# First two pairs of tiles from plain quadrants, keys and values as two offset streams, and weights split early: a gated mix of two linear attentions on one Trainium2 core

## The chip, the cores and the metric

The kernel runs on one core of one Trainium2 chip. The metric is the device time of one execution in microseconds. Engines are named as in the profile: PE (TensorE) multiplies, PEld loads its stationary operand, DVE (VectorE), ACT (ScalarE) and POOL (GpSimd) work on elements, and SP (SyncE) issues every transfer from one queue (SPq), in program order.

## The reference

A sequence of S = 2048 rows of D = 576 goes through two linear-attention blocks with 32 heads of 18, and a gate mixes the results. Block A maps queries and keys by elu + 1, block B by a learned projection and two softmaxes. Neither is causal, so each block needs one state over all rows (keys times values, and the sum of keys) before the first query can be answered.

```python
pq, pk = phi(q), phi(k)                  # A: phi(t) = (t > 0 ? t + 1 : exp(t)) + 1e-6
kv = einsum("bhsd,bhse->bhde", pk, v); z = einsum("bhsd->bhd", pk)
o = einsum("bhqd,bhde->bhqe", pq, kv) / (einsum("bhqd,bhd->bhq", pq, z)[..., None] + 1e-6)
a = o @ A_wo
pq, pk = q @ w_phi, k @ w_phi            # B: per head, then
phi_q = concat([softmax(pq), softmax(-pq)]); phi_k = concat([softmax(pk), softmax(-pk)])
...
g = sigmoid((x * gate_w).sum(-1, keepdims=True))
return g * a + (1 - g) * b
```

## The kernel before

The rows are cut into 16 tiles of 128, taken as 8 pairs. Matmuls run on fp32r operands; to keep fp32 precision each operand is split into a high part (an ACT copy) and a low part (a subtraction of that copy on DVE or POOL), and a product is made of high times high, high times low and low times high.

The work has three phases. Phase A projects keys and values of block A for pair 0 to 7 and adds each pair to the state in PSUM (`kv_a`, matmuls in L217). Phase B does the same for block B (`kv_b`). The query phase projects queries for both blocks, normalizes, transposes and makes the output (L156 projections, L652 numerators, L682 output).

Keys or values of a pair are made by a Winograd form of Strassen's scheme (`wino`, matmuls in L359): x and the weight are cut into 2 x 2 quadrants of 288, and seven products replace eight. A product is 7 matmuls of 128x288, so keys or values of one pair take 49. The price is in sums: `x_ops` makes four sums of quadrants per pair on DVE (L257 to L268) and splits seven operands (`x_op`: copy on ACT L237, subtractions on POOL L238 and L239); `w_ops` does the like for a weight (sums L313 to L322; `w_op`: L293 on ACT, L294 and L295 on DVE); and results are added back on DVE (L369).

W is a tile of 18 blocks of 1440 columns: seven blocks for keys, seven for values, and what is not yet used holds other things; the seven operands of pair 1 lie there at first. The operands of x (tiles xo, ten buffers of 640 columns) are written to DRAM when made (L274, `xd`) and read back in phase B (`x_back`, L286) by 56 loads of 320 KB.

The first pairs: x tiles and the four quadrants of the keys' weight are loaded in turn, `x_ops(0)`, `w_ops` and `x_ops(1)` are woven, then keys of pairs 0 and 1, then the values' weight, then values of both. From pair 2 on keys and values of a pair are woven product by product. In phase B the last two pairs do keys together, then `load_w` loads and splits the query weight of A (WAq, L121 to L124), then both pairs' values.

Then comes the change of phase: masked states `kta` (L504), the output weight of B loaded and split (L121 to L124), and `ma_units`, which multiplies A's state with A's output weight into MA (matmuls L540 and L543, high part on ACT L544, low part on DVE L546 and L548); these are woven with the query units of the first tile. Block B's state becomes `ktb`, z_b and kb (L702 to L725). In the query phase each tile adds 1 to its two gate columns on DVE (L558).

The framework's scheduler reorders instructions of each engine; `tc.high_priority(offset=AHEAD)` pulls the Winograd copies and adds ahead. The order on each engine is fixed when the kernel is built.

## Time and profile before

| | |
|---|---|
| median of 3 runs | 626.22 us (626.06 to 630.88) |
| the profiled execution | 630.87 us |
| its span in the trace | 629.2 us |
| mean granted clock of PE | 0.986 of full |
| busy: PE, DVE, ACT, POOL | 589.0, 490.5, 256.0, 244.4 us |

The profile shows one execution. The stretches of its trace are given from the start of the span; "granted clock" is the share of full speed (2.4 GHz) that the chip allowed PE in a stretch. A matmul's busy time holds its waiting in PE's pipeline, so full pace is read from how many matmuls a stretch holds, not from the mean of one.

### The profile page before, as it was taken

The page shows a single profiled execution, that of the slowest core. Times are in us where ns is not written, and L with a number is a line of the kernel's source. Part 1 is how long each engine was busy: PE and PEld are TensorE (multiplying, and loading weights), DVE is VectorE, ACT ScalarE, POOL GpSimd, SP SyncE. Part 2 cuts the span into 40 slices and gives each one's busy share as a digit, 9 for nine tenths or more (in the row PEclk, how much of TensorE's full clock was granted, in tenths as well). Part 3 has the DMA queues.
Part 4 walks back from the last instruction along what each step waited for, and adds up shares of the span by engine and source line. Part 5 has one row for each costly group of instructions (what it writes and reads, how often), then busy time and mean ns, then how long its engine had stood idle before and what let it go on. Part 6 is the DMA issues. An engine that isn't in the chain of part 4 may idle for free.

```text
span 629.2 us, 12059 instructions
## 1 busy us (share of the span) xinstructions
PE 589.0 (94%) x4786; PEld 570.5 (91%) x4786; DVE 490.5 (78%) x817; ACT 256.0 (41%) x541; POOL 244.4 (39%) x226
## 2 busy tenths in 40 slices
PE   2788999999999899998998799999999999999997
PEld 2778999999999899997887599999999999999997
DVE  5999564959678558676979986999899898989920
ACT  5456456556333333453333334343332434332331
POOL 5958764840022203469526212333234442322300
PEclk9799999999999899999999989999999999999999
DMA  8855666666855454143102000111010110000001
GB/s 303 292 202 203 257 220 203 207 213 220 272 168 178 120 160 155 46 133 94 45 18 78 22 22 20 41 41 41 20 41 21 41 41 20 20 20 20 13 26 39
DMA packets 29292, 67.56 MB, mean 107 GB/s; under 512 B 3232, under 2 KB 4384, under 8 KB 29236
## 3 DMA queue, kind: packets, MB, share of 16 engines
q1 hardware_dynamic: 29236, 66.79, 32.0%
q8 instruction: 38, 0.62, 0.4%
q14 instruction: 18, 0.15, 0.1%
HBM read 43.70 MB, written 23.07 MB: 106 GB/s over the span
## 4 chain that ended last, share of the span: by engine, by line
PE 69%; DVE 16%; DMA 2%; ACT 2%; POOL 1%; issue 1%; SPq 0%; DVEq 0%; POOLq 0%; ACTq 0%
PE yz L359 25%; PE pq L156 16%; PE bk L682 15%; PE tr L652 4%; PE bk L217 3%; PE tr L627 2%; DVE dd L577 1%; PE yz L340 1%; DVE row L180 1%; DVE row L576 1%; DVE gg L558 1%; DVE W L616 1%; PE tr L620 1%; DVE uw L203 1%; DVE mm L185 1%
## 5 line engine op out<-in xcount | busy, mean ns | idle before, releaser
L359 PE MATMUL yz<-W,xo 128*128 128x288 f32 (+1 forms) x1386 | 202.6, 303 | 14.0 <-ACT W L293 6.4
L359 PEld LDWEIGHTS yz<-W,xo 128*128 128x128 f32 (+1 forms) x1386 | 192.2, 194 | 17.9 <-ACT W L293 6.6
L156 PE MATMUL pq<-W,xh 128*128 128x288 f32 (+1 forms) x576 | 128.8, 305 | 3.0 <-DVE uw L193 2.4
L156 PEld LDWEIGHTS pq<-W,xh 128*128 128x128 f32 x576 | 96.1, 191 | 5.3 <-DVE uw L193 1.8
L156 PE MATMUL pq<-W,xl 128*128 128x288 f32 (+1 forms) x320 | 94.1, 299 | 0.0
L203 POOL TENSOR_TENSOR uw<-uw,rs 128x1152 f32<-128x1152 f32 x16 | 34.2, 2154 | 97.5 <-DVE rs L198 85.0
L682 PE MATMUL bk<-W,ath 128*128 128x288 f32 x288 | 64.1, 302 | 1.8 <-DVE W L616 1.5
L156 PEld LDWEIGHTS pq<-W,xl 128*128 128x128 f32 x320 | 61.0, 191 | 0.5 <-issue 0.4
L682 PE MATMUL bk<-W,vo 126*128 126x288 f32 x384 | 59.5, 297 | 0.0
L364 ACT ACTIVATE sc<-yz 128x288 f32<-128x288 f32 x96 | 37.6, 406 | 47.4 <-PE yz L359 44.0
L194 ACT ACTIVATE uw<-uw 128x1152 f32<-128x1152 f32 x32 | 37.2, 1164 | 47.1 <-DVE uw L193 47.0
L103 POOL TENSOR_TENSOR xl<-xraw,xh 128x640 fp32r<-128x640 f32 x16 | 25.8, 1614 | 78.4 <-ACT xh L102 78.3
L682 PEld LDWEIGHTS bk<-W,vo 126*128 126x128 f32 x384 | 53.4, 188 | 0.0
L369 DVE TENSOR_TENSOR row<-yz,sc 128x288 f32<-128x288 f32 x48 | 21.5, 450 | 40.5 <-PE yz L359 22.7
L563 POOL TENSOR_TENSOR row<-row,z_a 128x576 f32<-128x576 f32 x16 | 30.1, 1882 | 58.4 <-DVE row L180 58.4
L196 DVE TENSOR_REDUCE ss<-uw 128x64 f32<-128x1152 f32 x32 | 42.8, 1344 | 10.0 <-ACT uw L194 9.9
L682 PEld LDWEIGHTS bk<-W,ath 128*128 128x128 f32 x288 | 47.4, 189 | 2.3 <-ACT W L615 1.7
L682 PE MATMUL bk<-W,atl 128*128 128x288 f32 x160 | 47.5, 298 | 0.0
L238 POOL TENSOR_TENSOR xo<-xs,xo 128x256 fp32r<-128x256 f32 x28 | 26.9, 961 | 30.0 <-ACT xo L237 27.0
L652 PE MATMUL tr<-W,kb_h 126*126 126x256 f32 (+1 forms) x160 | 33.0, 285 | 1.9 <-DVE W L616 0.9
L569 POOL TENSOR_TENSOR row<-row,den 128x576 f32<-128x576 f32 x16 | 19.1, 1191 | 37.2 <-issue 16.9
L293 ACT ACTIVATE W<-st 128x864 fp32r<-128x864 f32 x28 | 25.6, 924 | 18.1 <-DVE st L313 5.2
(170 smaller groups left out, 1140.9 us busy)
## 6 DMA issues: line engine op xcount, KB each, us to landing
xo<-xd SPq DMA_DIRECT2D x50, 320.0 KB
xd<-xo SPq DMA_DIRECT2D x49, 320.0 KB
xr<-xq SPq DMA_DIRECT2D x16, 384.0 KB
xraw<-xT SPq DMA_DIRECT2D x16, 320.0 KB
out<-row SPq DMA_DIRECT2D x16, 288.0 KB
xd<-W SPq DMA_DIRECT2D x7, 320.0 KB
st<-wAk SPq DMA_DIRECT2D x4, 432.0 KB
st<-wAv SPq DMA_DIRECT2D x4, 432.0 KB
```

The lines of the kernel that those rows point to most:

```text
L103: eng.tensor_tensor(xl, raw, r(xh), op=ALU.subtract)
L156: PE.matmul(dst, xx[:, j, :], W[:, w, c0:c0 + n], start=(i == 0), stop=(i == len(steps) - 1))
L194: A.activation(uw, uw, AF.Exp)
L196: V.tensor_reduce(ss, uw.rearrange("p s (h d) -> p (s h) d", d=DH), op=ALU.add, axis=AX.X)
L203: eng.tensor_tensor(u3, u3, rs[:, :, None].to_broadcast([P, 64, DH]), op=ALU.mult)
L238: G.tensor_tensor(dst[:, 3:5], raw[:, 0:2], r(dst[:, 0:2]), op=ALU.subtract)
L293: A.activation(T[:, 0:3], raw, AF.Copy)
L359: PE.matmul(dst, x[:n, i], w[:n, j], start=(first and m == 0), stop=(m == 6), skip_group_check=True)
L364: A.activation(s, y, AF.Copy)
L563: G.tensor_tensor(zw, f[:, :D], z_a, op=ALU.mult)
L652: PE.matmul(dst, kk[:n, i, :w], uu[:n, i, :256], start=(m == 0), stop=(m == 5))
L682: PE.matmul(po[:, :HB], l, w, start=(i == 0), stop=(i == len(steps) - 1))
```

## The change

1. Keys and values of pairs 0 and 1 come from plain quadrants (`plain`, 8 block products of 7 matmuls per pair, 224 in all, line 425 of the changed kernel). `x_op` now splits two halves with one instruction per engine; four weight blocks for keys and four for values are split, their 32-row tail on POOL. The Winograd sums of the weights (`t_ops`) come after. For phase B only the first operand tiles of these pairs are stored; `x_late` loads x again and makes the others at steps 8 and 25.
2. From pair 2 on keys and values are two streams that step by one product each, values four steps behind (`LAG`). Other work hangs on numbered steps (`task`). x operands are three tiles of 1280 columns and one of 640 per pair, from four and two buffers; they come back by 24 loads of 640 KB and 8 of 320 KB.
3. `pre_split` loads and splits WAq and woB in phase B and stores both parts in DRAM (18 stores); at the end they are loaded straight into W. `kta` is made in phase B, and the units of MA stand in the steps of the last four values products, their low part made by POOL (L508, L510) from a second ACT copy. The gate's +1 goes from DVE to ACT, one scale of the last pair from POOL to DVE.

```diff
     def x_op(dst, raw):
-        A.activation(dst[:, 0:3], raw, AF.Copy)
-        G.tensor_tensor(dst[:, 3:5], raw[:, 0:2], r(dst[:, 0:2]), op=ALU.subtract)
-        G.tensor_tensor(dst[64:96, 2], raw[64:96, 2], r(dst[64:96, 2]), op=ALU.subtract)
+        A.activation(dst[:, :, 0:3], raw, AF.Copy)
+        G.tensor_tensor(dst[:, :, 3:5], raw[:, :, 0:2], r(dst[:, :, 0:2]), op=ALU.subtract)
+        G.tensor_tensor(dst[64:96, :, 2], raw[64:96, :, 2], r(dst[64:96, :, 2]), op=ALU.subtract)
...
+        return p1.tile([P, 1280], F32R, name="xo", bufs=4)
...
+    def x_late(i):
+        tiles = [xo_tile(), xo_tile(), xs_tile()]
+        r0, r1 = x_load(2 * i), x_load(2 * i + 1)
+        for t, raw in zip(tiles, sums(r0, r1)):
+            x_op(as_op(t), raw)
+        x_keep(i, tiles)
...
+    def plain(ops, ks, c, then=None):
...
+        for h in range(2):
+            ys = {}
+            for a in range(2):
+                for i in range(2):
+                    for t in range(2):
+                        if a == 0:
+                            ys[i, t] = y_tile()[:, :HB]
+                        x, w = ops[i][2 * t + a], T[2 * a + h]
+                        for m, (p, q) in enumerate(((0, 0), (0, 3), (1, 1), (1, 4), (3, 0), (4, 1), (2, 2))):
+                            n = 96 if p == 2 else P
+                            PE.matmul(ys[i, t], x[:n, p], w[:n, q], start=(a == 0 and m == 0), stop=(m == 6),
+                                      skip_group_check=True)
...
+                A.activation(MA[:, j, c], pm[:, :HB], AF.Copy)
+                mr = row_tile()[:, :HB]
+                A.activation(mr, pm[:, :HB], AF.Copy)
+                if j < 4:
+                    G.tensor_tensor(MA[:, 5 + j, c], mr, r(MA[:, j, c]), op=ALU.subtract)
...
+    def pre_split(src, hi, lo):
+        raw = wraw_tile()[:src.shape[0], :src.shape[1]]
+        nc.sync.dma_start(raw, src)
+        t = pw.tile([P, 2, 578], F32R, name="ws")[:src.shape[0], :, :src.shape[1]]
+        A.activation(t[:, 0], raw, AF.Copy)
+        G.tensor_tensor(t[:, 1], raw, r(t[:, 0]), op=ALU.subtract)
+        for k, m in enumerate((hi, lo)):
+            if m is not None:
+                a = t.shape[0] - m.shape[0]
+                nc.sync.dma_start(m, r(t[a:, k]))
...
-    weave(x_ops(0, o0, x00 + x01), w_ops(wa, AKS), x_ops(1, o1, x1))
-    weave(keys(0, o0, AKS, phi_elu), keys(1, o1, AKS, phi_elu))
-    weave(w_ops(w_raw(wAv), AVS))
-    weave(values(0, o0, AVS), values(1, o1, AVS))
...
+    x_op(as_op(o0[0]), x0[0])
+    w_op(4, ak[0], G)
+    x_op(as_op(o0[1]), x0[1])
+    w_op(5, ak[2], G)
+    for t, raw in zip(o1, x1):
+        x_op(as_op(t), raw)
+    w_op(2, ak[1], G)
+    w_op(10, ak[3], G)
...
+    weave(plain(plains, [4, 2, 5, 10], lambda i, t, h: row_half(cs[i][t], h)))
...
+    for n in range(n_all + LAG):
...
+        if n < n_all:
+            next(K)
+        if n % 7 == 3 and n + 4 < n_all:
+            x_next(*pair_of(n + 4))
+        m = n - LAG
...
+        if m >= 0:
+            next(V2)
+        for fn in events.pop(n, []):
+            fn()
...
-        V.tensor_scalar(gg, gg, 1.0, None, op0=ALU.add)
+        A.activation(gg, gg, AF.Copy, bias=1.0)
```

The start on PE, before: yz is the PSUM tile of a product, xo the operands of pair 0, W alone stands for a weight block with an operand of pair 1.

```order
L359 MATMUL yz<-W,xo 128x288 x7
L359 MATMUL yz<-W 128x288 x4
L359 MATMUL yz<-W,xo 128x288 x7
L359 MATMUL yz<-W 128x288 x4
L359 MATMUL yz<-W,xo 128x288 x7
L359 MATMUL yz<-W 128x288 x7
```

Products of the two pairs alternate there. The same place in the changed kernel: both operands of every plain matmul lie in W; bk is the state in PSUM.

```order
L425 MATMUL yz<-W 128x288 x224
L217 MATMUL bk<-row,vo 57x54 x10
L217 MATMUL bk<-row,vo 38x36
L217 MATMUL bk<-row,vo 57x54 x10
L217 MATMUL bk<-row,vo 38x36
L367 MATMUL yz<-W,xo 128x288 x42
```

The products of both pairs, keys and values, now stand in one run ahead of the first state update, and Winograd products begin with pair 2.

Phase B on SP in the changed kernel: loads of pairs 6 and 7 (xd6, xd7), with WAd and WBd the split weights.

```order
L298 DMA xo_2920<-xd6_0_1286 128x1280
L298 DMA xo_2921<-xd6_1_1288 128x1280
L298 DMA xs1_2923<-xd6_3_1292 128x640
L298 DMA xo_2922<-xd6_2_1290 128x1280
L298 DMA xo_3107<-xd7_0_1502 128x1280
L298 DMA xo_3108<-xd7_1_1504 128x1280
L298 DMA xs1_3110<-xd7_3_1508 128x640
L696 DMA W_95<-WAd_507 128x578 x2
L298 DMA xo_3109<-xd7_2_1506 128x1280
```

Where seven loads of 640 columns stood for a pair, there are three of 1280 and one of 640, with the weights' own loads behind and between them. On PE, around the first use of xo_3107, which takes the buffer of xo_2728:

```order
L367 MATMUL yz_2946<-W_95,xo_2728 128x288 x7
L367 MATMUL yz_3134<-W_95,xo_2920 128x288 x7
L367 MATMUL yz_3045<-W_95,xo_2922 128x288 x2
L367 MATMUL yz_3056<-W_95,xs1_2729 128x288 x7
L367 MATMUL yz_3045<-W_95,xo_2922 128x288 x5
L367 MATMUL yz_3225<-W_95,xo_3107 128x288 x7
```

Between the last reading of the old tile and the first of the new stand 21 matmuls; the load can go only after the first of these places and must be there at the second.

MA's matmuls on PE before (L540), among query projections (L156) and behind the work on block B's state (L721):

```order
L721 MATMUL tr<-row,ath 72x8
L721 MATMUL tr<-row,atl 72x8
L540 MATMUL tr<-wraw,ath 128x288 x4
L156 MATMUL pq<-W,xh 128x288 x2
L156 MATMUL pq<-W,xl 128x288
```

They come in pieces of one to eight with projections between them. In the changed kernel they are L500 and L503 (wraw is A's output weight; xraw, xh and xl hold the masked states):

```order
L500 MATMUL yz<-wraw,xraw 128x288 x4
L367 MATMUL yz<-W,xo 128x288 x7
L500 MATMUL yz<-wraw,xraw 128x288
L500 MATMUL yz<-wraw,xh 128x288
L500 MATMUL yz<-wraw,xraw 128x288
L500 MATMUL yz<-wraw,xh 128x288 x5
L367 MATMUL yz<-W,xo 128x288 x7
L367 MATMUL yz<-W,xs_3110 128x288 x7
L500 MATMUL yz<-wraw,xh 128x288 x2
L500 MATMUL yz<-wraw,xl 128x288 x2
L503 MATMUL yz<-wraw,xl 64x288 x4
```

They moved from behind the work on block B's state to the last values products, ahead of the first query projection.

## Rows read from the trace of the kernel before

**Rows 1.** The page: busy time (share of the span) and instructions by engine.

```profile
PE 589.0 (94%) x4786; PEld 570.5 (91%) x4786; DVE 490.5 (78%) x817; ACT 256.0 (41%) x541; POOL 244.4 (39%) x226
```

**Rows 2.** Stretches: length, then PE, PEld, DVE, ACT, POOL, PEclk, DMA, GB/s.

```profile
0.00:60.00 60.00, 40.22 (x238) 36.50 (x239) 51.46 (x70) 32.45 (x62) 41.11 (x65) 0.94 0.71 251
60.00:210.00 150.00, 146.20 (x1398) 142.24 (x1397) 106.48 (x175) 74.76 (x156) 59.63 (x72) 1.00 0.64 214
...
280.00:288.00 8.00, 6.57 (x46) 5.86 (x44) 7.68 (x12) 5.40 (x11) 7.08 (x5) 1.00 0.64 186
288.00:360.00 72.00, 64.14 (x495) 57.12 (x495) 60.17 (x123) 24.06 (x56) 37.85 (x25) 0.98 0.15 44
...
400.00:580.00 180.00, 179.10 (x1383) 178.87 (x1381) 163.57 (x274) 62.76 (x145) 59.72 (x38) 1.00 0.09 30
```

**Rows 3.** Stretches of 10 us, the same columns.

```profile
20.00:30.00 10.00, 6.68 (x26) 5.57 (x26) 9.83 (x12) 5.45 (x11) 9.14 (x12) 0.74 0.94 310
...
220.00:230.00 10.00, 10.00 (x77) 10.00 (x76) 3.43 (x7) 2.48 (x6) 0.00 (x0) 1.00 0.50 143
...
340.00:350.00 10.00, 7.07 (x28) 4.70 (x26) 9.94 (x24) 3.76 (x11) 4.32 (x3) 0.83 0.21 63
```

**Rows 4.** A stretch, matmuls of L359 alone: PE, PEld, PEclk, DMA, GB/s.

```profile
0.00:55.20 55.20, 35.29 (x196) 31.94 (x197) 0.94 0.70 246
```

**Rows 5.** Timeline of the start: start, duration, engine, line, [idle before].

```profile
0.81 0.38 SPq L243 DMA_DIRECT2D xr<-xq  x1
...
3.75 0.94 ACT L237 ACTIVATE xo<-xr 128x384 fp32r<-128x384 f32 x2 [1.67 <-DMA xr<-xq]
...
4.35 0.72 POOL L238 TENSOR_TENSOR xo<-xr,xo 128x256 fp32r<-128x256 f32 x1 [0.58 <-ACT xo L237]
...
5.16 0.45 POOL L239 TENSOR_TENSOR xo<-xr,xo 32x128 fp32r<-32x128 f32 x1
...
14.05 1.33 PE L359 MATMUL yz<-W 128*128 128x288 f32 x4 [5.17 <-ACT W L237]
...
23.66 0.53 PE L359 MATMUL yz<-W 128*128 128x288 f32 x2 [2.42 <-POOL W L238]
```

**Rows 6.** Groups by shape on POOL: busy us, mean ns of one, idle before.

```profile
L238 POOL TENSOR_TENSOR xo<-xs,xo 128x256 fp32r<-128x256 f32 x28 | 26.9, 961 | 30.0 <-ACT xo L237 27.0 <-POOL xo L239 1.9
...
L239 POOL TENSOR_TENSOR xo<-xs,xo 32x128 fp32r<-32x128 f32 x28 | 17.8, 635 | 2.2
```

**Rows 7.** Groups by shape on DVE, the same columns.

```profile
L294 DVE TENSOR_TENSOR W<-st,W 128x576 fp32r<-128x576 f32 x28 | 24.1, 860 | 10.7 <-ACT W L293 10.5
...
L203 DVE TENSOR_TENSOR uw<-uw,rs 128x1152 f32<-128x1152 f32 x16 | 22.9, 1431 | 0.2
...
L369 DVE TENSOR_TENSOR row<-yz,sc 128x288 f32<-128x288 f32 x48 | 21.5, 450 | 40.5 <-PE yz L359 22.7 <-ACT sc L364 17.6
...
L558 DVE TENSOR_SCALAR gg<-gg 128x2 f32<-128x2 f32 x16 | 16.8, 1052 | 0.0
...
L295 DVE TENSOR_TENSOR W<-st,W 32x288 fp32r<-32x288 f32 x28 | 16.0, 571 | 0.6
...
L268 DVE TENSOR_TENSOR xs<-xr,xs 128x384 f32<-128x384 f32 x8 | 6.9, 868 | 0.9 <-POOL xo L239 0.8
...
L546 DVE TENSOR_TENSOR W<-tr,W 128x288 fp32r<-128x288 f32 x8 | 3.5, 442 | 0.0
...
L504 DVE TENSOR_TENSOR ath<-bk,row 57x54 f32<-57x54 f32 x8 | 1.7, 212 | 4.0 <-POOL ath L493 3.9
```

**Rows 8.** Chain of waits from 270 to 380: start us, length us, what.

```profile
280.49 3.74 DMA xraw<-xT
```

**Rows 9.** Groups by shape on PE: the matmuls that make MA.

```profile
L540 PE MATMUL tr<-wraw,ath 128*128 128x288 f32 x28 | 9.6, 462 | 2.2 <-DVE W L546 1.2 <-DVE kb_l L725 1.0
...
L543 PE MATMUL tr<-wraw,atl 128*64 128x288 f32 x16 | 2.4, 419 | 0.0
...
L540 PE MATMUL tr<-wraw,atl 128*128 128x288 f32 x4 | 1.9, 556 | 0.0
```

More of the change, by code (lines that the diff above doesn't have):

```diff
@@ new lines, in tile_gated_mix, with pair_of, x_next @@
+    t1 = st_tile()
+    weave(t_ops(*[ak[k] for k in range(4)], AKS, t1, t1, ak[1], ak[2]))
+    ts = [st_tile() for _ in range(4)]
+    weave(t_ops(*[av[k] for k in range(4)], AVS, *ts))
+    pair_kv(0, kv_a)
+    later = list(range(2, NP))
+    ops, made = {}, {}
+    n_a = 7 * len(later)
+    n_all = n_a + 7 * NP
+    def pair_of(n):
+        return ("a", 2 + n // 7) if n < n_a else ("b", (n - n_a) // 7)
+    def x_next(ph, i):
+        if ph == "a":
+            tiles = xo_tiles()
+            ops[ph, i] = seven(tiles)
+            weave(x_ops(i, tiles))
+        else:
+            ops[ph, i] = x_back(i)
@@ new lines, in open_b, with bk_half @@
+    def open_b():
+        nonlocal px, pw
+        pa.release()
+        px = ctx.enter_context(tc.tile_pool(name="px", bufs=2, side="right", reuse_waits="tile"))
+        pw = tc.alloc_tile_pool(name="pw", bufs=2, side="right", reuse_waits="tile")
+    def bk_half(n):
+        if n == 0:
+            t1 = st_tile()
+            b11, b12, b21, b22 = folded
+            w_op(BKS[0], b11)
+            w_op(BKS[1], b21)
+            made["bk"] = t_ops(b11, b12, b21, b22, BKS, t1, t1, b12, b21)
+            for _ in range(2):
+                next(made["bk"])
+        else:
+            weave(made["bk"])
+            w_op(BKS[6], folded[3])
@@ new lines, in bv_load, with bv_part @@
+    def bv_load():
+        made["bv"] = {k: w_raw(wBv, k) for k in (0, 2, 1, 3)}
+    def bv_part(n):
+        bv = made["bv"]
+        if n < 2:
+            w_op(BVS[n], bv[2 * n])
+        if n == 1:
+            t1 = st_tile()
+            made["bvt"] = t_ops(*[bv[k] for k in range(4)], BVS, t1, t1, bv[1], bv[2])
+            next(made["bvt"])
+        if n == 2:
+            weave(made["bvt"])
+            w_op(BVS[6], bv[3])
+    px = pw = None
+    for k, i in enumerate(later):
+        task(7 * k + LAG + 2, lambda i=i: pair_kv(i - 1, kv_a))
```

327 lines of the change are left out of this document (180 added, 147 removed).

## The prediction

> **What bounds the kernel now.** I read the busy line of the page first [rows 1]. The reader is to see that TensorE (PE) is busy 589.0 of 629.2 us, so only 40 us of the span have no matmul in them, and that VectorE (DVE) comes next with 490.5. Then the stretches [rows 2]: from 60 to 210 us PE has 146.20 of 150.00, from 400 to 580 it has 179.10 of 180.00. Nothing is to be had there except by taking matmuls away. The loss lies in two places. From 0 to 60 us PE has 40.22, and from 288 to 360 us, between the last values product and the first output product, it has 64.14 of 72.00 while DVE has 60.17.
>
> Busy time hides a second loss, since a matmul that goes slowly is busy too. At 220 to 230 us there are 77 matmuls in 10.00 us [rows 3], 130 ns from one to the next; that is my full pace. The products of the first two pairs are 196 matmuls (two pairs, keys and values, 49 each) and are done at 55.20 us [rows 4]. At 130 ns they would take 25.5. So the start costs 29.7 us beyond its own matmuls, and it is the largest single thing a change can attack.
>
> The timeline of the start says why [rows 5]. The first transfer is issued at 0.81, the first copy begins at 3.75. At 14.05 PE has waited 5.17 us for the second pair's first x operand, which ScalarE (ACT) copies late, behind sums and weight blocks of the Winograd form, and at 23.66 it has waited 2.42 us for the POOL subtraction in L238. From 20 to 30 us there are only 26 matmuls, and the granted clock is 0.74 [rows 3]: between the levels 2.4 and 1.2 GHz, PE having waited just before.
>
> **The change part by part.** All terms are against the profiled execution, 630.87 us, which is the slowest of the three runs shown and 4.65 over their median of 626.22; 1.67 us of it lie around the span.
>
> *Start: -10 us.* The plain quadrants need no sums, but 224 matmuls in place of 196: +28 × 130 ns = +3.6 us. By the order of the changed kernel the first four groups of seven need one x tile each, tile after tile; from the fourth tile on the 196 matmuls that follow are free of POOL. So the end is the time of the fourth tile on POOL plus 25.5. An x tile is now one copy and two POOL subtractions over both halves. POOL's durations for half a tile are 0.72 and 0.45 us when DVE is idle [rows 5] and 0.961 and 0.635 on the mean [rows 6]. For both halves: from below 1.98 (0.72 and 0.45 differ by 0.27 for 128 more elements, so 0.18 of it is fixed; 512 elements make 1.26 and 256 make 0.72), from above 2 × (0.961 + 0.635) = 3.19. I take 2.4, nearer to the rows with DVE idle, since DVE has little to do before 10 us. The first copy ends at 3.75 + 0.94 = 4.69. Four tiles are 9.6, and the tails of two weight blocks on POOL (0.45 us for 128 elements, so about 0.8 for 288) 1.6: 15.9 us, with the bounds 12.6 (no tail in front) and 19.4. Then 25.5, and for a spell at the lower clock 1.7: the 0.74 from 20 to 30 cost 2.6 [rows 3], and I expect one that is shorter. This gives 43.1 against 55.2, so -12. I give 2 back to DVE, which has to make eight sums of weight blocks and split them behind the plain products. It has 51.46 us of work in the first 60 [rows 2], and 14 of them go or move later: 12 Winograd adds × 0.450 = 5.4; eight sums of x at up to 0.868 = 6.9; six tails × 0.571 = 3.4, less what contention keeps [rows 7]. About 37 us of work from 6 us on ends at 43 or 44, beside the last plain product: hidden, with nothing to spare. Range -13 to -4.
>
> The Trainium skill, page "SBUF — State Buffer", section "Who interferes with whom", says that a DVE instruction with two SBUF inputs contends with a GpSimd instruction that reads SBUF, and that the loser waits out the whole instruction. The rows agree that there is contention (0.72 alone, 0.961 on the mean), though the difference is 0.24 and not a whole DVE subtraction. By that rule the eight POOL subtractions would each wait for one DVE split; this is the second rival.
>
> *The middle, 60 to 288 us: 0.* The sums of the first two pairs come here, made late, with four more loads of x: 8 × 0.868 = at most 6.9 us on DVE, which has 106.48 of 150 [rows 2], so they are covered. Splitting the query and output weights early is nine ACT copies, nine POOL subtractions and 18 stores in phase B, where ACT and POOL are under half busy. If a store that waits for POOL holds SP's queue, the loads behind it are late; this is counted below. Range -3 to +5: PE has 3.8 us of idle to win, and +5 if DVE's late sums delay the Winograd adds.
>
> *Loads of phase B: +5.* Before, ten tiles of 640 columns came back by loads of 320 KB, and the order leaves some 90 matmuls or more between a tile's last reading and the first reading of its successor. Now four tiles of 1280 come back by 640 KB each. In the order of the changed kernel the tightest of the 24 loads has 21 matmuls to land in (the fence shows it: after the last row with xo_2728 come 7, 2, 7 and 5 others, then xo_3107), 2.7 us; two have 29 (3.8), one has 35 (4.6), the other 20 have 40 or more (5.2 and up). Landing: the first transfer, 384 KB, took 3.75 - 0.81 = 2.94 us [rows 5]; one of 320 KB took 3.74 from issue to landing with others in flight [rows 8]. At the 310 GB/s of the start [rows 3] 384 KB are 1.24 us of bytes, so 1.7 are fixed; 640 KB alone are then 1.7 + 2.1 = 3.8. From above, twice the 3.74 is 7.5. I take 4.8, one more us for a neighbour in flight, nearer to the row with the first transfer. The stalls are 2.1 + 2 × 1.0 + 0.2 = 4.3, and 0.7 for SP's queue, in which each load stands behind a wait for PE and behind the weight stores. Range +1 (3.8) to +28 (7.5: 4.8 + 2 × 3.7 + 2.9, and 13 on the other 20).
>
> *Between values and output, 288 to 360 us: -7.* PE has 7.86 us without a matmul here. From 340 to 350 us DVE is busy 9.94 of 10 and PE 7.07, at 0.83 of full clock [rows 3]: DVE sets the pace. The change takes from DVE the lo parts of MA (8 × 0.442 and two of the smaller form, 4.4), the eight masks of kta and three smaller (11 × 0.212 = 2.3), and in this stretch three or so of the gate adds (3 × 1.052 = 3.2). It puts one scale of uw on DVE (1.431). Together 8.5 less [rows 7]. The matmuls for MA, 9.6 + 1.9 + 2.4 = 13.9 us [rows 9], are not removed but stand earlier, behind the last keys product, where they cover the softmax of the last pair. PE's work is the same, so the gain is at most its idle time, 7.9, plus the 1.7 that the 0.83 cost, plus 1.4 of idle from 280 to 288 [rows 2]. I take most of the idle time. Range -11 to -2; if that cover is not needed, because query projections covered it before, only a DVE chain made shorter by 2 remains.
>
> *Gate adds in the query phase: -0.5.* The other 13 × 1.052 us leave DVE, but PE is busy 179.10 of 180.00 there [rows 2]; ACT, under half busy, takes them. Range 0 to -2.
>
> Sum: -10 + 0 + 5 - 7 - 0.5 = -12.5, so 618.4 us for an execution like the profiled one, and 613.7, say 614, for the median.
>
> **The rivals.**
> 1. *The loads starve PE (slower).* If a 640 KB load takes 7.5 us, twice the 3.74, the term for phase B is +28 and not +5: 614 + 23 = 637. For it: the 3.74 was measured where 186 GB/s were moved, well under the 310 of the start [rows 2, 3], and SP issues two or three loads in a row when a pair's tiles come free. Against it: the first 384 KB took 2.94 [rows 5]. It decides from a landing of about 7 us on; below 6 the kernel is still faster.
> 2. *POOL bounds the start.* If each of the eight subtractions waits for a DVE split of 0.860 [rows 7], the fourth tile is done at 15.9 + 6.9 = 23 and the plain products at 50, with DVE done before them: the start gains 5 us, 614 + 5 = 619. For it: the wait for L238 at 23.66. Against: the 0.24.
> 3. *The middle stretch is a chain, not a load on DVE.* Then -7 becomes -1: 620. For it: the sums, their copies and the reductions follow each other through four engines. Against: DVE at 9.94 of 10.
> 4. *All covers hold.* Start -12, loads +1, stretch -11: 614 - 2 - 4 - 4 = 604.
> That the change does not do what it says is small: the order shows 224 plain matmuls in front and the MA matmuls among the last values products.
>
> **How the numbers follow.** About 1%, 6.3 us, is what a measurement of this kernel can tell from no change: faster is under 620, slower over 632.5. Forecast 0.49 (its own range 606 to 621, nine tenths of it under 620), rival 1 0.12, rival 2 0.14, rival 3 0.13, rival 4 0.12. Faster: 0.44 + 0.12 + half of the 0.27 of rivals 2 and 3 = 0.70. Slower: nearly all of rival 1, 0.11. The rest, 0.19, is no change. The range goes from 600, somewhat under rival 4, to 631, which leaves out rival 1.
>
> **What would show it.** Right: the 224 plain matmuls done by 42 to 46 us; first output product some 12 us earlier than now; in phase B short waits of PE for a transfer of xo, 3 to 7 us in all. Wrong: waits for xo<-xd over 15 us (rival 1), a POOL queue without a gap until 23 us (rival 2), PE idle again for 7 us between values and output with DVE under 85% (rival 3).

## The result, and the profile after

Measured side by side, the changed kernel takes 631.55 us (median of 20 executions, 628.29 to 633.71) and the kernel before 628.74 (20 executions, 626.06 to 632.86). The ratio is 1.0038, 95% interval 1.0019 to 1.0056: about 2.4 us slower, against a forecast of 12 us faster. The profiled execution took 630.74 us, so it stands next to the one of before (630.87), and the two traces show where a gain and an equal loss lie. The traced executions are 0.13 us apart and the medians 2.81, so most of the 2.4 us stands in no stage of these two traces.

The page of the changed kernel, busy line and chain of waits by engine:

```profile
PE 594.9 (95%) x4814; PEld 576.8 (92%) x4814; DVE 473.2 (75%) x776; ACT 260.8 (41%) x547; POOL 248.7 (40%) x200
...
PE 70%; DVE 13%; DMA 5%; issue 2%; ACT 2%; POOL 1%; SPq 0%; POOLq 0%; ACTq 0%; DVEq 0%
```

PE has 28 matmuls more [rows 1], as planned, DVE 17 us less. The same stretches as [rows 2] (length, PE, PEld, DVE, ACT, POOL, PEclk, DMA share, GB/s):

```profile
0.00:60.00 60.00, 47.27 (x368) 44.26 (x369) 47.97 (x57) 32.25 (x52) 39.69 (x50) 0.94 0.62 218
60.00:210.00 150.00, 145.36 (x1291) 137.33 (x1290) 113.72 (x186) 78.20 (x151) 68.72 (x60) 1.00 0.69 241
280.00:288.00 8.00, 8.00 (x87) 7.68 (x87) 4.20 (x9) 1.54 (x4) 4.27 (x2) 1.00 0.87 273
288.00:360.00 72.00, 64.64 (x468) 61.01 (x466) 53.88 (x95) 31.15 (x70) 34.99 (x28) 0.93 0.17 50
400.00:580.00 180.00, 180.00 (x1391) 180.00 (x1390) 155.19 (x264) 65.18 (x157) 61.93 (x39) 1.00 0.09 29
```

In 60 us PE has done 368 matmuls and not 238: the start is much better. But from 60 to 210 it does 1291 and not 1398. Most of that difference is work that only moved: 88 small matmuls of the state update (L217) are done before 60 us, and 10 in the kernel before. The matmuls of the product line alone, before and after (PE, PEld, PEclk, DMA share, GB/s):

```profile
60.00:210.00 150.00, 119.47 (x858) 115.18 (x857) 1.00 0.64 214
```

```profile
60.00:210.00 150.00, 120.95 (x829) 111.64 (x828) 1.00 0.69 241
```

That is 29 products' matmuls fewer in more busy time, 3.8 us at 130 ns each; the busy time of the whole stretch (145.36 against 146.20) hides it. From 288 to 360 PE has as little as before, though DVE has 6 us less to do.

To see where the lead goes, marks are better than fixed stretches. I take four: the first Winograd matmul of pair 2 (1372 such matmuls are left in both kernels), the one with 784 left (as many as phase A has, 588, are done, and phase B's 784 are still to come), the one with 28 left, and the 50th matmul of the output product. Matmuls of the product line (L359, then L367) between the first three marks, before and after, columns PE, PEld, PEclk, DMA share, GB/s:

```profile
55.20:154.40 99.20, 82.37 (x590) 78.96 (x589) 1.00 0.66 226
154.40:282.20 127.80, 104.97 (x759) 102.68 (x758) 0.99 0.50 153
```

```profile
49.40:155.10 105.70, 87.77 (x588) 80.69 (x589) 0.99 0.69 246
155.10:284.30 129.20, 105.99 (x758) 101.36 (x757) 1.00 0.70 237
```

The same 588 matmuls take 99.2 us before and 105.7 after: a lead of 5.8 us at the first mark is a lag of 0.7 at the second. (At the first mark the changed kernel has 44 matmuls of the state update behind it, the kernel before 10, so the lead and the loss behind it are both a little larger than these numbers.) And from the 50th output matmul to the end (L682, then L848):

```profile
381.90:629.20 247.30, 127.98 (x846) 116.19 (x846) 1.00 0.09 30
```

```profile
384.60:628.90 244.30, 127.47 (x848) 116.10 (x846) 1.00 0.09 30
```

Here 3 us come back. Stages of all runs, from the marks in their traces (start: to the first mark; A, B, T: between the marks; Q: from the 50th output matmul to the end of the last matmul):

| kernel | start | A | B | T | Q | ratio to before |
|---|---|---|---|---|---|---|
| before | 55.2 | 99.2 | 127.7 | 99.8 | 243.5 | 1 |
| changed | 49.4 | 105.7 | 129.2 | 100.3 | 240.7 | 1.0038 |
| e1_ma_late | 50.1 | 106.9 | 129.7 | 102.4 | 240.2 | 1.0105 |
| e2_kv0_late | 42.5 | 116.4 | 131.2 | 96.2 | 240.6 | 1.0064 |
| e3_gate_dve | 49.8 | 105.9 | 129.7 | 98.6 | 242.6 | 1.0054 |
| e4_no_late | 50.1 | 103.9 | 133.2 | 93.9 | 240.6 | 1.0015 |
| e6_kv_whole | 50.0 | 106.4 | 128.5 | 93.9 | 241.2 | 0.9967 |
| e7_ma_lo_dve | 49.6 | 105.4 | 129.2 | 93.6 | 240.6 | 0.9983 |
| e8_ma_before | 49.6 | 106.0 | 133.5 | 102.4 | 240.2 | 1.0169 |
| b1_gate_act | 55.2 | 98.9 | 127.6 | 98.3 | 240.6 | 0.9953 |
| c1_whole_lo | 49.5 | 107.6 | 130.4 | 94.0 | 240.6 | 0.9971 |
| e9_lag0_lo | 49.4 | 109.2 | 127.8 | 93.8 | 240.6 | 0.9977 |
| e10_t_pool | 49.9 | 106.4 | 129.0 | 98.5 | 240.6 | 1.0031 |
| c2_lag0_whole_lo | 50.2 | 103.0 | 140.0 | 95.5 | 240.6 | 1.0041 |
| e11_phi_behind | 42.3 | 113.4 | 129.5 | 95.0 | 240.6 | 0.9979 |
| e12_all | 51.0 | 101.9 | 128.0 | 94.6 | 240.6 | 0.986 |
| c5_lag0_whole | 49.4 | 107.4 | 128.3 | 95.8 | 240.6 | 0.9953 |
| c4_lag0_whole_a | 49.7 | 103.4 | 138.4 | 94.6 | 240.6 | 1.0035 |

Each ratio is to the kernel before on the same chip in turn, with an interval of about 0.002 to each side (0.004 for e12). e4 and e12 leave work out, so their results are not those of the reference. Stages are those of one profiled execution, which can lie some us from the median (e7: 623.78 against 627.27); differences of a microsecond in one stage are not readings.

### The profile page after: what moved, and what is told of

Same layout as the page of the kernel before. It is cut to its first block, busy times and chain, and to the rows that moved or that the text cites. A ratio compares the mean times of both kernels' runs of the same rounds, so it can differ in the third digit from the quotient of the medians.

```text
span 628.9 us, 11973 instructions
## 1 busy us (share of the span) xinstructions
PE 594.9 (95%) x4814; PEld 576.8 (92%) x4814; DVE 473.2 (75%) x776; ACT 260.8 (41%) x547; POOL 248.7 (40%) x200
## 4 chain that ended last, share of the span: by engine, by line
PE 70%; DVE 13%; DMA 5%; issue 2%; ACT 2%; POOL 1%; SPq 0%; POOLq 0%; ACTq 0%; DVEq 0%
PE yz L367 20%; PE bk L848 19%; PE pq L156 17%; PE tr L818 4%; PE bk L217 3%; PE tr L793 2%; DMA xo<-xd 1%; DMA WAd<-ws 1%; DVE ss L196 1%; PE tr L786 1%; DVE W L306 1%; PE yz L348 1%; DMA xr<-xq 1%; DVE row L180 1%; DVE W L307 1%
## 5 line engine op out<-in xcount | busy, mean ns | idle before, releaser
L367 PE MATMUL yz<-W,xo 128*128 128x288 f32 (+1 forms) x1176 | 174.1, 301 | 2.9 <-DMA xo<-xd 2.1
L367 PEld LDWEIGHTS yz<-W,xo 128*128 128x128 f32 (+1 forms) x1176 | 160.9, 190 | 6.9 <-ACT sc L372 3.1
L156 PE MATMUL pq<-W,xh 128*128 128x288 f32 (+1 forms) x576 | 128.8, 306 | 4.7 <-DVE uw L193 3.4
L156 PEld LDWEIGHTS pq<-W,xh 128*128 128x128 f32 x576 | 97.2, 194 | 5.6 <-issue 2.6
L156 PE MATMUL pq<-W,xl 128*128 128x288 f32 (+1 forms) x320 | 94.6, 301 | 0.0
L103 POOL TENSOR_TENSOR xl<-xraw,xh 128x640 fp32r<-128x640 f32 x16 | 26.0, 1628 | 99.8 <-ACT xh L102 99.8
L848 PE MATMUL bk<-W,ath 128*128 128x288 f32 x288 | 64.5, 304 | 0.4 <-ACT row L849 0.4
L156 PEld LDWEIGHTS pq<-W,xl 128*128 128x128 f32 x320 | 61.9, 193 | 0.0
L848 PE MATMUL bk<-W,vo 126*128 126x288 f32 x384 | 60.4, 297 | 0.0
L203 POOL TENSOR_TENSOR uw<-uw,rs 128x1152 f32<-128x1152 f32 x15 | 32.0, 2153 | 60.2 <-DVE rs L198 43.2
L848 PEld LDWEIGHTS bk<-W,vo 126*128 126x128 f32 x384 | 53.8, 188 | 0.0
L372 ACT ACTIVATE sc<-yz 128x288 f32<-128x288 f32 x84 | 32.4, 407 | 47.7 <-PE yz L367 47.6
L848 PEld LDWEIGHTS bk<-W,ath 128*128 128x128 f32 x288 | 48.3, 193 | 0.6 <-ACT row L849 0.6
L848 PE MATMUL bk<-W,atl 128*128 128x288 f32 x160 | 48.1, 302 | 0.0
L377 DVE TENSOR_TENSOR row<-yz,sc 128x288 f32<-128x288 f32 x42 | 18.9, 450 | 35.6 <-PE yz L367 25.6
L425 PE MATMUL yz<-W 128*128 128x288 f32 (+1 forms) x224 | 34.2, 312 | 7.8 <-ACT W L305 5.8
L425 PEld LDWEIGHTS yz<-W 128*128 128x128 f32 (+1 forms) x224 | 32.1, 199 | 9.6 <-ACT W L305 5.8
L179 DVE TENSOR_SCALAR row<-row 128x576 f32<-128x576 f32 x32 | 25.1, 786 | 15.6 <-ACT row L178 15.3
```

The costliest lines, as they stand in the source:

```text
L103: eng.tensor_tensor(xl, raw, r(xh), op=ALU.subtract)
L156: PE.matmul(dst, xx[:, j, :], W[:, w, c0:c0 + n], start=(i == 0), stop=(i == len(steps) - 1))
L179: V.tensor_scalar(fx, fx, 1.0, EPS, op0=ALU.min, op1=ALU.add)
L203: eng.tensor_tensor(u3, u3, rs[:, :, None].to_broadcast([P, 64, DH]), op=ALU.mult)
L367: PE.matmul(dst, x[:n, i], w[:n, j], start=(first and m == 0), stop=(m == 6), skip_group_check=True)
L372: A.activation(s, y, AF.Copy)
```

## The experiments

**The stretch between values and output, and the gate.** The trace suggests at first that MA, standing in front, starves DVE. Timeline at the end of the values, changed kernel (start, duration, idle before):

```profile
302.75 1.39 POOL L716 TENSOR_TENSOR wob_x<-wraw,wob_y 96x576 fp32r<-96x576 f32 x1
303.20 0.41 ACT L678 ACTIVATE W<-yz 64x288 fp32r<-64x288 f32 x1
...
304.37 0.41 ACT L678 ACTIVATE W<-yz 64x288 fp32r<-64x288 f32 x1
...
304.82 1.19 PE L704 MATMUL tr<-xraw,row 128*128 128x108 f32 x4 [2.20 <-ACT W L678]
...
307.41 0.83 PE L156 MATMUL pq<-W,xh 128*128 128x288 f32 x2
...
313.23 0.76 DVE L185 TENSOR_REDUCE mm<-pq 128x32 f32<-128x576 f32 x1 [9.44 <-PE pq L156]
```

Two things are to be seen: DVE idles 9.44 us until the first projection is there, and PE waits 2.20 us until ACT has evacuated the last MA product, whose PSUM the next pool takes over. The first was my theory.

e1 puts MA behind the first projections:

```diff
-                pm = y_tile()
+                pm = tr_tile()
...
-    for k in range(LAG):
-        task(n_all + k, lambda: (next(mau), next(mau)))
...
-    weave(qu0)
+    weave(qu0, mau)
```

> The changed kernel with MA's matmuls put back behind the first two query projections, woven with the rest of the first query unit; the second query's x is loaded after them. Theory: in the changed kernel the 13.9 us of MA stand in front of the first projection, DVE idles 9.4 us and is then full from 325 to 368, so what was to be saved there is lost. Moved back, the first projection starts at about 294 and not at 307, DVE's idle of 9.4 goes, the spell at half clock at 307 to 311 goes, and the time falls by 4 to 8 us against the changed kernel (ratio to before 0.991 to 0.997). Rival: the stretch is bounded by the chain through the state of block B and the first queries, wherever MA stands: within 1.5 us of the changed kernel (ratio 1.001 to 1.006).

It took 634.81 us, ratio 1.0105 (1.0080 to 1.0130): slower than the changed kernel by 0.7%, more than the rival allowed. The theory fell, with a reservation: the second x tile had to wait for the buffers of the masked states. e8 removes that reservation (kta made at the end, in tiles of its own, as before).

> The changed kernel with masked states and MA made as before: kta at the end on DVE in tiles of its own, MA woven with the first query unit, both first x tiles loaded at once (in the earlier run with MA behind the projections the second x tile had to wait for the masked states' buffers). Theory: with MA in front DVE starves for 9.4 us; here the first projection starts near 295 and the output's 100th matmul comes 3 to 6 us earlier than in the changed kernel (ratio 0.994 to 0.999). Rival: DVE's sum of work decides, and 4 us of it come back: equal or up to 4 us slower (ratio 1.003 to 1.010).

638.75 us, ratio 1.0169 (1.0143 to 1.0195): 1.3%, or 8 us, above the changed kernel, so the theory falls and the rival's 4 us are exceeded. With the low parts on POOL in both, MA in front is a gain: T is 100.3 and not 102.4. The rest lies mostly in B, 129.2 against 133.5, although the masks are gone from it in e8; why it grows is not shown. DVE's idle time there was no loss.

e7 takes the other thing:

```diff
-                mr = row_tile()[:, :HB]
-                A.activation(mr, pm[:, :HB], AF.Copy)
                 if j < 4:
-                    G.tensor_tensor(MA[:, 5 + j, c], mr, r(MA[:, j, c]), op=ALU.subtract)
+                    V.tensor_tensor(MA[:, 5 + j, c], pm[:, :HB], r(MA[:, j, c]), op=ALU.subtract)
...
```

> The changed kernel with the low parts of MA made on DVE from PSUM again, without the second ACT copy and the POOL subtraction. Theory: the ten second copies (4.1 us) and ten subtractions (about 11 us) queue on ACT and POOL in front of the last pair's scale, the memset and the release of PSUM, and are what PE waits for at 302 to 305 and then runs at half clock; DVE has room there. 2 to 5 us faster than the changed kernel (ratio 0.996 to 1.001), the first query projection at 303 to 305 and not 307. Rival: DVE is full from 325 on and what is added to it before is only moved: within 1 us (ratio 1.002 to 1.005).

627.27 us, ratio 0.9983 (0.9959 to 1.0007), 0.55% under the changed kernel. PE in the stretch of its trace, where it no longer waits:

```profile
298.17 2.16 PE L503 MATMUL yz<-wraw,xl 128*64 128x288 f32 x16
300.16 2.26 PE L217 MATMUL bk<-uw,vo 128*57 128x108 f32 x44
302.35 0.69 PE L702 MATMUL tr<-xraw,row 128*128 128x108 f32 x4
```

And the clock, 300 to 310 us, first in the changed kernel, then in e7 (columns as in [rows 3]):

```profile
300.00:310.00 10.00, 7.80 (x69) 7.63 (x66) 1.61 (x6) 5.78 (x12) 7.04 (x8) 0.73 0.11 33
```

```profile
300.00:310.00 10.00, 9.85 (x107) 9.53 (x104) 4.36 (x11) 5.70 (x12) 2.94 (x2) 1.00 0.22 65
```

The wait cost twice: 2.2 us, and a spell at 1.2 GHz behind it, with the granted clock at 0.50 for at least 5 us. The changed kernel again:

```profile
306.00:311.00 5.00, 5.00 (x24) 5.00 (x23) 0.00 (x0) 1.52 (x3) 1.55 (x1) 0.50 0.31 88
```

T falls from 100.3 to 93.6, so the gain that e7's theory promised is there. Its mechanism is not. ACT evacuates the last MA product in e7 as late as in the changed kernel, where this began at 304.37:

```profile
304.53 0.41 ACT L676 ACTIVATE W<-yz 64x288 fp32r<-64x288 f32 x1 [0.55 <-DVE W L508]
```

PE goes on at 302.35 all the same. So the release of that PSUM did not come earlier by the copies left out; PE's next tile no longer hangs on it. Which tile the next pool takes over is settled when the kernel is built, and why this edit changes it is not shown.

e3 puts the gate's +1 back on DVE (`V.tensor_scalar(gg, gg, 1.0, None, op0=ALU.add)`), b1 moves it to ACT in the kernel before and changes nothing else.

> The changed kernel with the gate's +1 back on DVE. Theory: the query phase from the 50th output matmul to the end took 240.4 us in the changed kernel and 243.2 before, and the gate adds are the cause: with them back it takes 243 again, and the stretch before it loses 1 to 3 more: 3 to 5 us slower than the changed kernel (ratio 1.008 to 1.012). Rival, as predicted: PE is full there and the adds are hidden: within 1 us (ratio 1.003 to 1.005).

> The kernel before with only the gate's +1 moved from DVE to ACT. Theory: DVE is near its limit in the query phase (163.6 of 180 us), and the 16 adds of 1.05 us delay the chains that release PE: 2 to 4 us faster than before (ratio 0.994 to 0.997). Rival, as predicted: PE is full there, 0 to 1 us (ratio 0.998 to 1.000).

e3: 632.21 us, ratio 1.0054 (1.0035 to 1.0073), whose interval meets that of the changed kernel: unclear in time, but Q is 242.6 and not 240.7. b1: 625.51 us, ratio 0.9953 (0.9930 to 0.9975), Q 240.6 and not 243.5. So the adds do cost 3 us in the kernel before, as b1's theory had it; in the changed kernel they cost 2 us of Q, and the time does not tell.

**The start.** The plain products ended when they were expected to. Timeline of PE:

```profile
5.77 0.61 PE L425 MATMUL yz<-W 128*128 128x288 f32 x1 [5.77 <-ACT W L305]
...
14.95 12.35 PE L425 MATMUL yz<-W 96*128 96x288 f32 x86 [0.41 <-POOL W L240]
28.59 13.34 PE L425 MATMUL yz<-W 128*128 128x288 f32 x98 [1.29 <-ACT row L429]
...
44.25 0.52 PE L217 MATMUL bk<-row,vo 128*57 128x54 f32 x12 [1.87 <-ACT vo L429]
47.61 0.82 PE L217 MATMUL bk<-row,vo 128*57 128x54 f32 x10 [2.84 <-DVE row L180]
...
49.44 7.02 PE L367 MATMUL yz<-W,xo 128*128 128x288 f32 x42
```

The last plain matmul is out before 42.4 us; then pair 0's state update waits twice, for a copy on ACT and for a feature map on DVE, and the first Winograd product stands behind it. e2 moves this update to step 2.

```diff
-    pair_kv(0, kv_a)
...
+    task(2, lambda: pair_kv(0, kv_a))
```

> The changed kernel with the state update of pair 0 moved from in front of the first Winograd product to step 2. Theory: PE's two waits of 1.87 and 2.84 us behind the plain products come only from this update standing in front; Winograd products start near 43 instead of 49.4, and the time falls by 3 to 5 us (ratio 0.996 to 0.999). Rival: ACT's copies of the plain values, which queue behind an exponential that waits for DVE, hold four of the six PSUM tiles, so PE comes no further: under 1.5 us (ratio 1.002 to 1.005).

632.29 us, ratio 1.0064 (1.0048 to 1.0080). The Winograd products do start at 42.5, 7 us earlier, and at 784 left all of it is gone (158.8 against 155.1). The theory's gain in time does not come, and the rival's reason is out, since PE does come further. e10 takes four splits of weight sums from DVE to POOL:

> The changed kernel with the four splits of the values' weight sums (T) on POOL and not on DVE: 4 x (0.76 + 0.45) us leave DVE between 25 and 55 us, where POOL has room. Theory: the start is bounded by DVE, which ends its sums, splits and feature maps at 50 to 55 us though the plain products end at 42.4; the first Winograd product comes 2 to 4 us earlier than 49.4 and the 784th from the end 1 to 3 us earlier. Rival: POOL's subtractions slow DVE's by contention and nothing comes earlier (within 1 us).

630.99 us, ratio 1.0031 (1.0010 to 1.0051); first product at 49.9. Nothing comes earlier, as the rival said; that contention is the reason is not shown, since PE's waits there end with ACT's copies of the values (3.31 and 1.50 us). e11 queues the exponentials of the first two pairs behind the value copies on ACT, moves the update to step 2 and has e7's low parts:

```diff
+    with tc.issue_after(getattr(copies[-1], 'ins', copies[-1])):
+        for i in range(2):
+            done[i] = [phi_elu(c) for c in cs[i]]
```

> The changed kernel with MA's low parts on DVE, the feature maps of the first two pairs queued on ACT behind the copies of the plain values, and the state update of pair 0 moved to step 2. Theory: what holds the first Winograd product until 49.4 is not DVE's load but ACT's queue, in which exponentials that wait for a row buffer (freed by DVE) stand in front of the copies that free PSUM; now 44 Winograd matmuls stand behind the plain ones, the first at 42 to 43 us, with no wait over 1 us up to 55, and the 784th product from the end comes 4 to 6 us earlier than 154.9 (ratio 0.988 to 0.993). Rival: the stretch up to the 784th product is bounded by DVE's chains, so the lead is lost again there: 784th at 153.5 to 156, ratio 0.996 to 1.000.

627.83 us, ratio 0.9979 (0.9953 to 1.0006), no better than e7; the 784th product comes at 155.7, as the rival said. PE in its trace:

```profile
42.32 6.03 PE L367 MATMUL yz<-W,xo 128*128 128x288 f32 x44
51.47 1.34 PE L217 MATMUL bk<-row,vo 128*57 128x54 f32 x22 [3.12 <-DVE row L180]
55.93 1.34 PE L217 MATMUL bk<-row,vo 128*57 128x54 f32 x22 [3.12 <-DVE row L180]
```

PE runs ahead by 7 us and then waits twice for DVE's feature maps, with the clock down again, granted 0.52 in the stretch of 10 us around them:

```profile
50.00:60.00 10.00, 5.41 (x56) 5.20 (x56) 9.06 (x14) 3.35 (x7) 4.81 (x6) 0.52 0.76 279
```

So ACT's order was only the first of two queues; behind it stands DVE. One reason why DVE is late, contrary to my sum, is in the timeline of the changed kernel, first DVE and then POOL in the same place:

```profile
40.43 0.55 DVE L265 TENSOR_TENSOR xs<-xs,xr 128x384 f32<-128x384 f32 x1
40.90 0.55 DVE L266 TENSOR_TENSOR xr<-xr 128x384 f32<-128x384 f32 x1
...
43.75 1.07 DVE L265 TENSOR_TENSOR xs<-xs,xr 128x384 f32<-128x384 f32 x1
44.75 1.61 DVE L266 TENSOR_TENSOR xr<-xr 128x384 f32<-128x384 f32 x1
```

```profile
43.59 0.82 POOL L240 TENSOR_TENSOR xo<-xs,xo 32x256 fp32r<-32x256 f32 x1
44.49 1.46 POOL L239 TENSOR_TENSOR xo<-xr,xo 128x512 fp32r<-128x512 f32 x1
```

The same sum takes 0.55 us when POOL is idle (POOL works on no tile from 34 to 42 us) and 1.61 beside a POOL subtraction, ending 0.41 us after it: 44.49 + 1.46 = 45.95 and 44.75 + 1.61 = 46.36. Of the DVE instructions that begin between 24 and 50 us ten are over 0.1 us longer than the shortest of their shape, 6.7 us in all. POOL loses as well, 3.0 us there and 5.9 from 4 to 24 us. Here DVE begins first and POOL's subtraction, 1.27 us at its shortest, takes 2.00:

```profile
11.44 1.09 DVE L319 TENSOR_TENSOR st<-st 128x864 f32<-128x864 f32 x1 [1.29 <-DMA st<-wAk]
```

```profile
11.69 2.00 POOL L239 TENSOR_TENSOR W<-xr,W 128x512 fp32r<-128x512 f32 x1
```

In these rows the one that begins later is the one that waits. The first row shows another reason: up to 11.44 DVE stands idle, 1.29 us for the transfer of a weight block and 2.72 before that for ACT's copy of one.

**Phase A.** The stretch A whole, before and after (length, PE, PEld, DVE, ACT, POOL, PEclk, DMA share, GB/s):

```profile
55.20:154.40 99.20, 97.61 (x948) 94.67 (x947) 67.16 (x108) 54.16 (x117) 55.52 (x73) 1.00 0.66 226
```

```profile
49.40:155.10 105.70, 102.35 (x915) 96.41 (x913) 74.87 (x114) 57.54 (x113) 55.59 (x53) 0.99 0.69 246
```

Of the 6.5 us lost 1.8 are idle time of PE (3.4 against 1.6); the rest is busy time, with 33 matmuls fewer in it. DVE has 7.7 us more to do. By the trace the way from a product to a state update and back costs 0.25 us (94, 88 and 110 ns more than full pace at the two changes and the matmul behind, less 48), and from the first mark to the first projection there are 32 such returns in the changed kernel, 15 before: by this estimate 17 more returns are about 4 us. e6 holds each pair's update together:

```diff
+        k = 0 if kvf is kv_a else 1
+        m0 = kvf(*parts[k], last)
+        with tc.issue_after(m0):
+            kvf(*parts[k], GRP3[:-1])
+            kvf(*parts[1 - k])
```

> The changed kernel with each pair's state update held together on PE: its matmuls are queued behind the one whose operands come last, so PE changes between products and updates 44 times in phase A and 31 in phase B, not 61 and 34 (before: 33 and 23). Theory: a change there and back costs 0.25 us (94 + 88 + 110 - 48 ns by the trace), and the extra ones are most of what phase A lost: 20 changes fewer are 10 returns, 2.5 us faster than the changed kernel (ratio 0.999 to 1.001), the 784th product from the end at 152 to 153.5 us. Rival: the pieces filled gaps in which PE would have waited anyway: within 1 us (ratio 1.003 to 1.006).

626.84 us, ratio 0.9967 (0.9949 to 0.9985): faster than expected, but not where it was expected. A stays at 106.4 and T falls to 93.9, because the wait for PSUM goes, here too with the last MA product evacuated late, at 303.20, and PE going on at 302.16. In phase A the saved changes came back as waits: PE is busy 100.64 of 106.40 us, so 5.8 are idle and not 3.4. Waits of PE from 60 to 215 us (in total, times, longest):

```profile
PE yz L371 <- DVE row L381: 3.2, 5, 1.0
PE bk L217 <- DVE vo L381: 1.7, 1, 1.7
```

Both are Winograd adds on DVE. c1 joins e6 and e7 (both edits):

> The changed kernel with both of the edits that helped: each pair's state update held together, and MA's low parts on DVE. Theory: both gains came from one place, PE's wait of 2.2 us for the release of PSUM at 302 and the half clock after it; together they are hardly more than one alone (ratio 0.995 to 0.998). Rival: two separate gains, 4 us each: ratio 0.990 to 0.993.

627.22 us, ratio 0.9971 (0.9952 to 0.9990): no more than one alone, and no wait for PSUM in its trace either. Both gains are the same wait.

e4 leaves out the late operands (`stored[i] += stored[2][1:]` in place of loads, sums, splits and stores):

> The changed kernel without the late operands of the first two pairs: their four loads of x, eight sums, splits and six stores are left out, and phase B reads pair 2's stored operands in their place, so block B's state for these pairs is another one. Theory: the 6 us that phase A loses from 104 to 155 us come from these sums on a DVE that is full at 100 to 110 and 140 to 160: 4 to 6 us faster than the changed kernel (ratio 0.994 to 0.998), the 784th product from the end at about 150 us. Rival: they come from the two offset streams, whose state updates are cut into more pieces on PE: under 1.5 us (ratio 1.002 to 1.005).

629.75 us, ratio 1.0015 (0.9994 to 1.0037); A is 103.9 and B 133.2, together longer than before the edit. So A gets 1.8 of its 6.5 us back and B loses 4.0: at this offset leaving the late operands out gains nothing up to the last products. T falls to 93.9 here as well, without either of the two edits; its trace has no wait for PSUM there, so where that wait stands hangs on more than e6's and e7's edits. The offset itself, with e7's low parts:

> The changed kernel with MA's low parts on DVE and LAG = 0, so that keys and values of a pair step together as before. Theory: the offset of four steps costs phase A some 4 us, since state updates come in more pieces and Winograd adds of two pairs meet on DVE; without it the stretch from the 1372nd to the 784th product from the end takes 101 to 103 us and not 105.7 (before: 99.2), and the time is 2 to 4 us under that of the kernel with DVE's low parts alone (ratio 0.992 to 0.995). Rival: what phase A loses is DVE's late adds behind the sums and splits that came into this stretch, at any offset, and the softmax of the last pair is hidden less: 0 to 4 us slower than that kernel (ratio 0.998 to 1.005).

627.60 us, ratio 0.9977 (0.9954 to 1.0000): A 109.2, B 127.8. The rival holds for A; B comes back to what it was before. (LAG = 0 also takes away the steps that held MA; in the trace its matmuls stand among the last products all the same.) With whole updates one step later, and then without the late operands:

> The changed kernel with LAG = 0, each pair's state update held together and one step later, and MA's low parts on DVE: 34 changes between products and updates in phase A and 20 in phase B, as many as before (33 and 23). Theory: with the cuts and the late adds of the offset gone, phase A's stretch from the 1372nd to the 784th product takes 100 to 102 us (before 99.2) and the ratio is 0.988 to 0.992. Rival: the stretch stays above 104, ratio 0.995 to 0.999.

> The kernel with LAG = 0, whole state updates and DVE's low parts, which took 103.0 us from the 1372nd to the 784th product, now also without the late operands (phase B reads pair 2's for the first two pairs, so block B's state is another one). Theory: the 6.5 us that phase A loses against before (99.2) are the late operands' sums and splits (2 to 3) and the pieces and offset (about 3): the stretch takes 100 to 101.5 us. Rival: the late operands cost nothing where the streams are not offset: 102.5 to 103.5.

c2: 631.59 us, ratio 1.0041 (1.0020 to 1.0063), A 103.0 as the theory wanted, but B 140.0, so nothing is gained. e12: 619.29 us, ratio 0.9860 (0.9823 to 0.9897), A 101.9 and B 128.0. The two differ in the late operands alone. So here they cost 12 us, and nearly all of it in B, which neither theory had said. Two more runs vary the step, c5 with all updates at their old step, c4 with those of block A one later:

> The changed kernel with LAG = 0, whole state updates at their old step (two after the pair's last product) and MA's low parts on DVE; nothing left out. Theory: the offset costs in phase B (129.2 us from the 784th to the 28th product from the end, before 127.8; 127.7 at LAG 0) and the pieces in phase A (109.2 at LAG 0, 103.0 with whole updates one step later), so this one takes about 103 to 105 and 127.5 to 128.5 and is the fastest that computes all of it: ratio 0.988 to 0.993. Rival: whole updates at their old step wait for DVE's feature maps in phase A, which stays over 106: ratio 0.996 to 1.000.

> The same with the state updates of block A one step later (three after the last product), those of block B at two. Theory: phase A as in the earlier run with whole updates one step later (103), phase B free of its waits (3.3 us for DVE at the state update, 2.9 for a load of xo): ratio 0.988 to 0.993. Rival: the waits at the change from A to B come from block A's last update being late, and stay: 1.000 to 1.005.

c5: 625.80 us, ratio 0.9953 (0.9929 to 0.9976), A 107.4, B 128.3. c4: 630.23, ratio 1.0035 (1.0013 to 1.0056), A 103.4, B 138.4. With the late operands in, the later step only moves the wait from A to B. What PE waits for from the first mark to 157 us in c5:

```profile
PE bk L217 <- DVE row L180: 5.7, 4, 2.2
PE yz L352 <- ACT row L178: 1.7, 1, 1.7
```

and what it waits for DVE's feature maps (L180) from 50 to 300 us, in c2 and then in e12, with the eight sums gone:

```profile
PE bk L217 <- DVE row L180: 4.9, 5, 2.1
```

```profile
PE bk L217 <- DVE row L180: 1.1, 2, 0.6
```

In every version of the changed kernel that computes everything the product with 28 left comes at 284 to 293 us; before it was 282.2. Cut up, the updates cost PE its changes; whole, they wait for DVE.

## Why the prediction was wrong

By the stages of the two traces the terms came out as -5.8 (start, forecast -10), +6.5 and +1.5 (A and B, forecast 0 and, for the loads, +5), +0.5 (between values and output, -7) and -2.8 (from there to the end, -0.5).

*Start, -10.* The plain products end at 41.9 (43.1 was expected), in part by luck. POOL's first tile took 1.27 + 1.12 = 2.39 us (2.4 was taken), but the third and fourth took longer, and the fourth was done at 16.74 + 0.83 = 17.57 and not at 15.9; in return the spell at the lower clock, 1.7 us, did not come: the granted clock was 1.00 from 0 to 40 us. What failed is the sentence that DVE's work "ends at 43 or 44, beside the last plain product: hidden, with nothing to spare". The feature map that PE needs came at 47.6. The size of the work was right, 37.27 us busy from 6 to 47.6 (37 was taken), contention with POOL in it. Left out was the time in which DVE could not yet work, the 2.72 and 1.29 us up to 11.44. I had seen the contention and laid it on POOL alone; from 24 us on DVE loses more by it than POOL does. To the first mark the gain was 5.8. e2 and e11 bring that mark 7 us forward and gain nothing by it, since PE then waits for DVE.

*The middle, 0.* This step failed most. To 28 products left the lead of 5.8 became a lag of 2.1. I had costed only new work ("8 × 0.868 = at most 6.9 us on DVE, which has 106.48 of 150, so they are covered") and called it covered because DVE has room on the average. A DVE busy 76% of 150 us can still deliver each add late. e12 shows that this work is not covered: with LAG = 0 and whole updates one step later, leaving it out takes 12 us off (c2, 631.59, to 619.29). With the offset of four steps it takes off hardly anything (e4), so there the order counts too, which the sum left out: the two offset streams cut the state updates into pieces (32 returns for 15). That these cost about 4 us is an estimate that no run confirms: with whole updates (e6, c5) A stays above 106, and PE waits for DVE instead. An average share says nothing of who waits at which moment.

*Loads of phase B, +5.* The direction was right and the size smaller. PE's waits for them, and the two landings in the chain of waits:

```profile
PE yz L367 <- DMA xo<-xd: 2.1, 3, 1.1
```

```profile
174.25 4.80 DMA xo<-xd
...
262.06 3.78 DMA xo<-xd
```

One of 640 KB landed in 4.80 us, as was taken, one in 3.78, the lower bound (3.8). In the chains of the variants such loads took from 3.65 (e7) to 8.63 us (c5), so landings as long as rival 1's do occur; but PE's waits for them stay under 5 us in all in every run, and rival 1, which had them over 15, is out.

*Between values and output, -7.* Measured, the term is +0.5. The step that failed is that PE's idle time there would go: it is 7.36 us from 288 to 360 (7.86 before), with DVE busy 75%. New in it is the wait of 2.20 us for PSUM, with the half clock behind it. Without this wait (e7) T is 6.2 shorter than before, near the forecast, but still not by the idle time:

```profile
288.00:360.00 72.00, 65.25 (x506) 60.99 (x505) 62.57 (x113) 29.56 (x65) 30.31 (x20) 1.00 0.17 49
```

6.75 us are idle there, 1.1 less than before; PE gets through 506 matmuls in place of 495, at a granted clock of 1.00 and not 0.98. So the nearness of -6.2 to -7 is luck. That MA in front of the projections is worth something is what e1 and e8 show against the changed kernel; that it is the cause of the 6.2 is not shown, since no run has MA behind them with its low parts on DVE.

*Gate adds, -0.5.* Mis-sized: Q is 2.8 us shorter, and b1 gives 3 us in time. "PE is busy 179.10 of 180.00 there" was read as covering everything; that DVE is on the path outside that stretch, and at its block changes, is the likely reason and was not tested.

Of the signs that were to show it, the plain products came in time, but the first output product comes 10.6 us later (370.55 against 359.95) and not 12 earlier, and PE's waits for xo are 2.1 us and not 3 to 7. The sign for rival 3, PE idle again for 7 us between values and output with DVE under 85%, came true, and with it the term that this rival gave (-1, measured +0.5). The sign for rival 2, a POOL queue without a gap until 23 us, came true as well, but not the rival: behind the fourth tile POOL works on the tails of weight blocks, and the products end at 41.9, not at 50. Rivals 1 and 4 did not come. "No change" came from a lead that was given back. The median of before, 626.22 of three, was low: 628.74 of twenty.

What stays open: how the loss of phases A and B divides between the late operands, DVE's contention with POOL and the order of its queue. That POOL's subtractions are moved away from DVE's sums was not tried, nor the late operands at another place with LAG = 0. Of the versions that compute everything, four lie under the kernel before with their whole interval: b1 (before, gate on ACT) and c5 (changed, LAG = 0, whole updates, low parts on DVE), both at 0.9953, then e6 (0.9967) and c1 (0.9971).

## What to carry to other kernels

A lead on the bounding engine is worth only what the engine that feeds it can follow: before costing a faster start, add up the feeder's work to the first point where the leader must wait for it, with the durations that it has beside its neighbours, and with the time in which it cannot start yet. Compare kernels by marks (so many matmuls of one line left), not by busy share, nor by a bare count: 145.36 and 146.20 of 150 us hid 29 matmuls of products, and the count of all matmuls showed 107, most of which had only moved. And when a new wait goes with an edit, see whether what it waited for really came earlier.
